# Last unit's attention values with tokens in rows, two loads cut in halves, and three PSUM banks exchanged, in a pooled-attention and cosine-gated MLP kernel

## The chip, the cores and the metric

The kernel runs on one core of a Trainium2 chip. The metric is the time of one execution on the device in microseconds; the median of several runs is taken. In the profile PE is TensorE, PEld its weight loads, DVE VectorE, ACT ScalarE, POOL GpSimd and SP the engine that issues DMAs only.

## The reference, cut to what matters

There are 8 batches, 8 heads, 576 positions of 64 dimensions. Keys and values are averaged over groups of 8 positions (72 groups), q attends to them, and the result, as 4608 tokens of 512, goes through a layer of 2048 hidden units with the activation h * cos(h).

```python
k_p = k.reshape(B, H, Sp, pool, D).mean(axis=3)
v_p = v.reshape(B, H, Sp, pool, D).mean(axis=3)
scores = scale * np.matmul(q, k_p.transpose(0, 1, 3, 2))
attn = softmax(scores)                      # max subtracted, 1e-9 in the sum
x = np.matmul(attn, v_p)                    # as [4608 tokens, 512]
h = x @ w_in                                # 512 -> 2048
out = (h * np.cos(h)) @ w_out               # 2048 -> 512
```

## The kernel before, in words

**Stages.** The tokens are cut into nine tiles of 512. A tile has an up stage (h, its cosine, the product g) and a down stage (g times w_out). The attention of batch t + 1 is computed inside the down stage of tile t; batch 0 has a prologue of its own. A batch has 576 tokens and a tile 512, so tile 1 holds the last 64 tokens of batch 0 (the unit `REST`) and the first 448 of batch 1. The order of every engine's instructions is the order in which the program writes them (`manual_schedule`); a wait stands only where data or a buffer need it.

**Units of attention.** For batches 0 and 1 a batch's first 512 tokens are four units `us[0]` to `us[3]`: two blocks of 256 tokens for heads 0 to 3, then the same for heads 4 to 7. A unit's output is two of the four 128-row chunks of `xT` (tokens along the free dimension): `us[0]` and `us[1]` fill chunks 0 and 1, `us[2]` and `us[3]` chunks 2 and 3. The up matmuls contract over these chunks (`ki`).

**Prologue (batch 0).** k, v and q are loaded in a form in which matmuls with a 0/1 matrix `groups` do the pooling: `pool_k_mm` (L178), `pool_v_mm` (L186, copied out to `vz` on DVE, L188). q is transposed on PE (L215, L216). For each unit: `scores` (PE L234, Exp on ACT L241), `sums_first` (matmuls with ones, L313, then Ln and Exp(-x) on ACT, L317 and L318, which give the inverse of the softmax's sum), `values_then` (PE L327, multiplication on DVE into `xT`, L329). `warm_up` (L527) is matmuls on constants. From batch 2 on units of 128 tokens for all heads go through `values_rows`: matmuls with the tokens in the output's rows (L296), with the sum as a 65th column, a reciprocal (L299) and a multiplication (L301) on DVE, and a transposing DMA into `xT`.

**Up stage.** `up_mm` (L354) computes pairs `fp` of 128-wide blocks of h, 8 matmuls a pair; `up_bank` gives the pair's PSUM bank; Sin on ACT (L364), product on DVE (L368). Of the first two pairs of a tile the matmuls on chunks 0 and 1 are written ahead of those on chunks 2 and 3. In tile 0 the pairs go through `banks[0]`, `banks[2]`, `banks[1]` in turn; in later tiles through `banks[0]`, `banks[2]`, `banks[1]` and the two `obanks`, in the order of pairs 0, 4, 1, 5, and so on.

**Down stage of tile 0.** 64 matmuls (L371) into four accumulators, with a list `fill` of other work and the place at which each stands: the attention of `REST` and of batch 1 (`S_` scores, `V_` values: PE L269, ACT L275 and L276, DVE L280), sums of weight blocks on DVE (`put_weights`, L387) for the later tiles' down stages, which use fewer products, and the copies of the accumulators (`down_out`, DVE L375, then stores on SP). The second accumulator pair lies in `banks[1]`; `us[3]`'s values are in `banks[0]`, and their multiplication is held back to place 57.

**Loads and pooling on POOL.** All loads of k, v, q, w_in and w_out except the first of k are issued from POOL's queue (L96, L115, L124, L130); each takes one of eight semaphores, so a load waits for the one eight before it. From batch 2 on POOL pools k and v with additions (L157, L163, L166, L169). w_in comes in four blocks of 512 columns, used by pairs 0 and 1, 2 and 3, 4 and 5, 6 and 7.

Of the kernel before, what the change touches and what calls it, by code (L numbers as in the profile page):

```python
# [10 lines left out]
BF16 = mybir.dt.bfloat16  # L11
# [9 lines left out]
def kernel(  # L21
# [9 lines left out]
    nc = tc.nc  # L31
    B, H, S, D = q.shape
# [5 lines left out]
    KCH = d_model // 128  # L38
# [10 lines left out]
    REST = (SEG[2], (0, H))  # L49
# [10 lines left out]
    msb = ctx.enter_context(tc.tile_pool(name="msb", bufs=3))  # L60
    psum = ctx.enter_context(tc.tile_pool(name="psum", bufs=1, space=bass.MemoryType.PSUM))

    w_in_sb = [wpool.tile([128, KCH, 512], BF16, name=f"w_in_sb{i}") for i in range(4)]
    w_out_sb = [wpool.tile([128, 4, d_model], BF16, name=f"w_out_sb{i}") for i in range(4)]
    xT = wpool.tile([128, KCH, n_tokens], BF16, name="xT")
    g_sb = wpool.tile([128, FFCH, TILE], BF16, name="g_sb")
# [28 lines left out]
    def load_even(dst, b, src, j0=0, j1=KCH):  # L95
        nc.gpsimd.dma_start(out=dst[:, j0:j1].rearrange("p j t d -> p j (t d)"), in_=even_view(src, b, j0, j1))  # L96
# [23 lines left out]
        q_tile(b)  # L120
        load_even(staged["q", b], b, q)

    def load_w_in(cg):
        nc.gpsimd.dma_start(  # L124
            out=w_in_sb[cg],
            in_=moe_w_in[:, cg * 512:(cg + 1) * 512].rearrange("(k p) f -> p k f", p=128))


    def load_w_out(cg):
# [88 lines left out]
    def ex_col(u, i):  # L218

        (c0, n), (h0, nh) = u  # L220
        return (i // 2 % 2 * (nh // 2) + i // 4 * 2 + i % 2) * n

    def scores(b, u, pair):
        scores_mm(b, u, pair)
        scores_exp(b, u, pair)
# [59 lines left out]
        else:  # L285
            later.append(mul)

    def values_rows(b, u, pair):

        (c0, n), (h0, nh) = u  # L290
        ex = att.pop(("ex", b, u))
        ps = pair.rearrange("p b n -> p (b n)").rearrange("p (j w) -> p j w", w=2 * 128)
        for i in range(nh):
            pj, hp = divmod(i, 2)
            v_and_sum = vz[b % 2].rearrange("p j a d -> p j (a d)")[:, pj, hp * (3 * D - 1):hp * (3 * D - 1) + D + 1]
            nc.tensor.matmul(ps[0:n, pj, hp * (D + 1):(hp + 1) * (D + 1)], lhsT=ex[:, ex_col(u, i):ex_col(u, i) + n],  # L296
                             rhs=v_and_sum)
        inv = asb.tile([128, KCH, 2], FP32, name="inv_rows", tag="inv_rows", bufs=2)
        nc.vector.reciprocal(out=inv[0:n], in_=ps[0:n, :, D:D + 2])  # L299
        x = asb.tile([128, d_model], BF16, name="x_rows", tag="x_rows", bufs=4)  # L300
        nc.vector.tensor_tensor(  # L301
            out=x[0:n].rearrange("p (j a d) -> p j a d", j=KCH, a=2),
            in0=ps[0:n, :, 0:2 * (D + 2)].rearrange("p j (a w) -> p j a w", a=2)[:, :, :, 0:D],
            in1=inv[0:n].unsqueeze(3).to_broadcast([n, KCH, 2, D]), op=mybir.AluOpType.mult)
        nc.sync.dma_start_transpose(out=xT[:, :, b * S + c0:b * S + c0 + n], in_=x[0:n])

    def sums_first(b, u, cs):

# [33 lines left out]
    def up_bank(t, fp):  # L342
        i = list(up_order(t)).index(fp)
        if t < FIRST:
            return (banks[0], banks[2], banks[1])[i % 3]
        return (banks[0], banks[2], banks[1], obanks)[i % 4 if i < 7 else 0]

    def up_mm(t, fp, k0=0, k1=KCH):

        h = up_bank(t, fp)  # L350
        for j in range(2):
            fc = 2 * fp + j
            for ki in range(k0, k1):
                nc.tensor.matmul(h[j] if h is obanks else h[:, j, :], lhsT=w_in_sb[fc // 4][:, ki, fc % 4:512:4],  # L354
                                 rhs=xT[:, ki, t * TILE:(t + 1) * TILE],
                                 start=(ki == 0), stop=(ki == KCH - 1))

# [129 lines left out]
    load_even(staged["q", 0], 0, q, 0, 2)  # L487
    load_even(staged["k", 0], 0, k, 2, 4)
    load_even(staged["q", 0], 0, q, 2, 4)
    load_even(staged["v", 0], 0, v)  # L490
    identity = consts.tile([128, 128], BF16, name="identity")
    make_identity(nc, identity)
    dist, sign = [x.rearrange("p f n -> p (f n)").bitcast(FP32)[:, 0:ROW * Sp].rearrange("p (t n) -> p t n", t=ROW)
# [13 lines left out]

    kv_even_tiles(1)
    q_tile(1)
    for cg in range(3):  # L510
        load_w_in(cg)
    load_even(staged["k", 1], 1, k)
    load_even(staged["q", 1], 1, q, 0, 2)
    load_w_in(3)
    load_even(staged["q", 1], 1, q, 2, 4)
    load_w_out(0)
    load_even(staged["v", 1], 1, v)
# [6 lines left out]
    def warm_up(n, bank):  # L524

        for i in range(n):
            nc.tensor.matmul(bank, lhsT=warm[:, 0:128], rhs=warm)  # L527
# [16 lines left out]
    for put in (q_transpose_mm(0, banks[2][:, 0, :], 9, 14), q_transpose_mm(0, obanks[0], 14, 18)):  # L544
        put(vec)
    sums_first(0, us[1], obanks[1])
    warm_up(2, banks[1][:, 0, :])
    scores(0, us[2], banks[0])
    scores(0, us[3], banks[2])
    pool_v_mm(0, banks[1], 0, 2)  # L550
    sums_first(0, us[2], banks[0][:, 0, :])
    values_then(0, us[0], obanks[1])
    pool_v_mm(0, banks[1], 2, 4)
    values_then(0, us[1], obanks[0])
    sums_first(0, us[3], banks[2][:, 0, :])
    values_then(0, us[2], obanks[1])
    values_then(0, us[3], banks[1][:, 0, :])
    up_mm(0, 0, 0, 2)
    up_mm(0, 1, 0, 2)
    sin_tables()  # L560

    for t in range(NT):
# [35 lines left out]
        def S_(n, bank):  # L598
            return lambda: scores(b, us[n], banks[bank])
# [3 lines left out]
        def V_(n, bank, wait=None):  # L603
            return lambda: values(b, us[n], banks[bank], wait)
# [5 lines left out]
        if t < FIRST:  # L610

            mms = [(ms, 4 * cg + f) for cgs, mss in (((0, 2), (0, 1)), ((0, 2), (2, 3)), ((1, 3), (2, 3, 0, 1)))
                   for cg in cgs for ms in mss for f in range(4)]
            acc = [*obanks, banks[1][:, 0, :], banks[1][:, 1, :]]
            os = [msb.tile([128, 2, d_model], FP32, name="o_two", tag="o_two", bufs=2) for _ in range(2)]
            fill = [(2, lambda: scores(t, REST, banks[1])), (2, S_(0, 0)),
                    (4, lambda: put_weights(0, nc.vector, (1,))),
                    (8, lambda: pool_v_mm(1, banks[2])), (8, lambda: values(t, REST, banks[1])),
                    (8, lambda: put_weights(0, nc.vector, (3, 2))), (8, S_(1, 0)), (9, V_(0, 2)),
                    (18, lambda: put_weights(0, nc.vector, (4,))), (20, lambda: put_weights(1, nc.vector, (1,))),  # L620
                    (20, V_(1, 0)), (28, S_(2, 2)), (35, S_(3, 0)), (36, V_(2, 2)),
                    (38, lambda: put_weights(1, nc.vector, (3, 2, 4))), (44, V_(3, 0, later)), (57, lambda: later.pop()())]
# [123 lines left out]
```

## Time and profile before

| | us |
|---|---|
| median of 3 runs | 293.5 (293.22 to 293.76) |
| profiled execution | 293.22, of which the span from first to last instruction 291.4 |
| PE busy | 275.0 (94%) |
| DVE busy | 213.0 (73%) |
| ACT busy | 168.0 (58%) |
| POOL busy | 131.6 (45%) |

An engine's busy time is the union of its instructions. The chain that ended last, followed back from the end, is 85% PE. The prologue lies from 0 to 17.3 us (the first up matmul), tile 0's up stage to 33.6, its down stage to 53.6, and tile 1's up stage begins at 59.4.

### The profile page before, as it was taken

What the parts mean: (1) busy time and instruction counts of PE and PEld (TensorE: products, weight loads), DVE (VectorE), ACT (ScalarE), POOL (GpSimd) and SP (SyncE); (2) the same over time, 40 slices, a digit from 0 to 9 for tenths busy, and PEclk for the clock granted to TensorE, in tenths of its full rate; (3) what the DMA queues carried; (4) which work ended last, traced back from release to release, by engine and by line L of the source; (5) the groups of instructions that cost most, each with busy time, mean ns of one, the idle gap of its engine ahead of it and who ended that gap; (6) DMA issues with size and microseconds to landing.
All of it is one profiled execution on the core that took longest, in us unless ns stands there. A gap on an engine that the chain in (4) does not pass through costs nothing.

```text
span 291.4 us, 5864 instructions
## 1 busy us (share of the span) xinstructions
PE 275.0 (94%) x2356; PEld 185.6 (64%) x2378; DVE 213.0 (73%) x311; ACT 168.0 (58%) x201; POOL 131.6 (45%) x146
## 2 busy tenths in 40 slices
PE   7799999389999999999999999999999999999993
PEld 2555554135786578658865886588558855885682
DVE  5358775947985897589668966896689669846972
ACT  3786797226835683569356835684567456436600
POOL 8443016992079628980898089809930000000000
PEclk9999999869999999999999999999999999999999
DMA  7999999695825989979596959794570251006014
GB/s 157 197 207 211 212 205 159 90 188 85 139 55 53 151 161 201 139 143 198 89 153 111 213 91 161 138 191 77 110 157 3 55 122 42 2 13 130 2 36 109
DMA packets 56202, 36.13 MB, mean 124 GB/s; under 512 B 35440, under 2 KB 51312, under 8 KB 56176
## 3 DMA queue, kind: packets, MB, share of 16 engines
q0 software_dynamic: 18208, 18.07, 39.1%
q1 hardware_dynamic: 37328, 17.18, 29.0%
q10 hardware_dynamic: 640, 0.52, 0.8%
q8 instruction: 18, 0.29, 0.4%
q14 instruction: 8, 0.07, 0.1%
HBM read 36.70 MB, written 9.44 MB: 158 GB/s over the span
## 4 chain that ended last, share of the span: by engine, by line
PE 85%; DVE 5%; ACT 5%; DMA 2%; issue 2%; POOL 0%; POOLq 0%
PE bank L354 38%; PE obank L431 32%; PE obank L354 5%; PE bank L234 3%; DVE w L387 2%; DMA q_b<-in_q_dram 2%; PE bank L296 2%; ACT ex L241 2%; PE bank L431 2%; DVE xT L280 2%; PE bank L269 1%; ACT v_sb L275 1%; DVE o_two L375 0%; PE obank L178 0%; DVE g_sb L368 0%
## 5 line engine op out<-in xcount | busy, mean ns | idle before, releaser
L354 PE MATMUL bank<-xT,w_in_sb 128*128 128x512 bf16 x495 | 114.6, 383 | 6.8 <-DVE xT L280 5.8
L364 ACT ACTIVATE cos<-bank,half_pi 128x1024 f32<-128x1024 f32 x64 | 70.5, 1116 | 62.7 <-PE bank L354 62.7
L354 PEld LDWEIGHTS <-w_in_sb 128*128 128x128 bf16 x576 | 65.1, 114 | 64.8 <-DVE xT L280 6.3
L368 DVE TENSOR_TENSOR g_sb<-bank,cos 128x1024 bf16<-128x1024 f32 x64 | 76.9, 1220 | 35.0 <-ACT cos L364 35.0
L157 POOL TENSOR_TENSOR half_sums<-kv_st 72x512 f32<-72x512 bf16 x48 | 53.9, 1149 | 8.2 <-DMA kv_st<-in_k_dram 7.7
L241 ACT ACTIVATE ex<-bank 72x1024 bf16<-72x1024 f32 (+1 forms) x40 | 35.0, 931 | 31.8 <-PE bank L234 31.8
L431 PEld LDWEIGHTS <-g 128*128 128x128 bf16 x512 | 47.8, 98 | 5.8
L431 PE MATMUL obank<-w,g 128*128 128x256 bf16 x368 | 42.6, 273 | 0.0
L431 PEld LDWEIGHTS <-g_sb 128*128 128x128 bf16 x384 | 36.9, 98 | 6.4
L163 POOL TENSOR_TENSOR half_sums<-half_sums 72x512 f32<-72x512 f32 x24 | 30.0, 1272 | 0.0
L431 PE MATMUL obank<-w_out_sb,g_sb 128*128 128x256 bf16 x240 | 28.9, 273 | 0.0
L397 DVE TENSOR_TENSOR g<-g_sb 128x1024 bf16<-128x1024 bf16 x32 | 21.9, 685 | 0.3
L710 POOL COPY gate<-g 1x1 bf16<-1x1 bf16 x5 | 0.9, 179 | 42.0 <-DVE inv_rows L299 42.0
L301 DVE TENSOR_TENSOR x_rows<-bank,inv_rows 128x512 bf16<-128x512 f32 x24 | 16.6, 691 | 0.8
L280 DVE TENSOR_TENSOR xT<-bank,inv 64x256 bf16<-64x256 f32 x14 | 5.9, 422 | 15.4 <-ACT inv L276 15.3
L431 PE MATMUL obank<-w_out_sb,g 128*128 128x256 bf16 x112 | 15.6, 273 | 0.0
L431 PE MATMUL obank<-w,g_sb 128*128 128x256 bf16 x128 | 15.3, 273 | 0.0
L354 PE MATMUL obank<-xT,w_in_sb 128*128 128x512 bf16 x64 | 15.1, 380 | 0.0
L234 PE MATMUL bank<-qT,kk 64*72 64x128 bf16 (+2 forms) x288 | 12.4, 222 | 0.6 <-DVE xT L280 0.5
L234 PEld LDWEIGHTS <-kk 64*72 64x72 bf16 x288 | 8.7, 111 | 5.7 <-issue 3.4
L332 ACT ACT_TABLE_LOAD x9 | 11.5, 1283 | 0.9 <-PEq L730 0.7
L335 ACT ACT_TABLE_LOAD x9 | 11.5, 1283 | 0.2
(101 smaller groups left out, 274.0 us busy)
## 6 DMA issues: line engine op xcount, KB each, us to landing
out_dram<-o_two SPq DMA_DIRECT2D x64, 128.0 KB, 2.4
kv_st<-in_v_dram POOLq DMA_DIRECT2D x8, 576.0 KB, 12.3
kv_st<-in_k_dram POOLq DMA_DIRECT2D x7, 576.0 KB, 7.7
q_b<-in_q_dram POOLq DMA_DIRECT2D x6, 576.0 KB, 7.7
w_in_sb<-in_moe_w_in_dram POOLq DMA_DIRECT2D x4, 512.0 KB, 13.9
w_out_sb<-in_moe_w_out_dram POOLq DMA_DIRECT2D x4, 512.0 KB, 18.2
q_b<-in_q_dram POOLq DMA_DIRECT2D x4, 288.0 KB, 12.6
g_sb<-in_k_dram SPq DMA_DIRECT2D x1, 576.0 KB, 3.5
```

The lines of the kernel that those rows point to most:

```text
L157: nc.gpsimd.tensor_tensor(out=s[:, h:h + 2], in0=x[:, h:h + 2, 0:4, :], in1=x[:, h:h + 2, 4:8, :], op=ADD)
L163: add(out=s[:, h:h + 4, 0:2, :], in0=s[:, h:h + 4, 0:2, :], in1=s[:, h:h + 4, 2:4, :], op=ADD)
L234: nc.tensor.matmul(pair[:Sp, bank, c:c + n].rearrange("p (g n) -> p g n", n=64), lhsT=kk[b % 2][half[r], key_slot(b, h0 + i, r), 0:Sp], rh ...
L241: nc.scalar.activation(out=ex[:, 0:nh * n].rearrange("p (a n) -> p a n", a=2), in_=pair[:Sp, :, 0:nh * n // 2], func=ACTF.Exp, scale=scale ...
L280: nc.vector.tensor_mul(out=x_out(b, u, half[hp]), in0=cols(pair[half[hp], hp, :], u), in1=cols(inv[half[1 - hp]], u))
L301: nc.vector.tensor_tensor(out=x[0:n].rearrange("p (j a d) -> p j a d", j=KCH, a=2), in0=ps[0:n, :, 0:2 * (D + 2)].rearrange("p j (a w) -> ...
L332: nc.scalar.preload_act_table_set("natural_log_exp_and_others")
L354: nc.tensor.matmul(h[j] if h is obanks else h[:, j, :], lhsT=w_in_sb[fc // 4][:, ki, fc % 4:512:4], rhs=xT[:, ki, t * TILE:(t + 1) * TILE] ...
L364: nc.scalar.activation(out=c, in_=ps, func=ACTF.Sin, bias=half_pi[:, :1])
L368: nc.vector.tensor_mul(out=o, in0=ps, in1=c)
L397: nc.vector.tensor_tensor(out=out[:, f0:f1], in0=x, in1=y, op=op)
L431: mms.append(lambda bank=bank, first=first, g=g, w=w, fc=fc, p=p: nc.tensor.matmul(bank[p], lhsT=g(fc, p), rhs=w(fc), start=(first and fc ...
```

## The change

1. **v of batch 0 in two loads**, for the first and the last four heads. The two calls of `pool_v_mm`, which already take half of the heads each, then wait for one load each. The first moves ahead of the scores of `us[2]` and `us[3]`, and the values of `us[0]` and `us[1]` ahead of the second. The two warm-up matmuls there go.
2. **`us[3]` of batch 0 with tokens in rows.** `value_rows` is the old `values_rows` without its DMA, and takes a unit of 256 tokens and four heads as two blocks of 128 tokens. `x_transpose_mm` transposes the four 128x128 blocks on PE into PSUM, and ACT copies them into `xT`. `us[3]`'s sums, its Ln and Exp, go. The first four up matmuls stand between the values and the transposes.
3. **w_in's first block in two loads** (rows of chunks 0 and 1, of chunks 2 and 3), each a tile of its own.
4. **Banks.** Tile 0's up pairs go through `banks[1]`, `banks[0]`, `banks[2]`. In its down stage `banks[0]`, `[1]`, `[2]` stand where `[2]`, `[0]`, `[1]` stood: the second accumulator pair is in `banks[2]`, `us[2]`'s values in `banks[0]`, `us[3]`'s in `banks[1]`. Later tiles keep their order of banks.

```diff
+    WIN = ((0, 0, 2), (0, 2, 4), (1, 0, 4), (2, 0, 4), (3, 0, 4))
+    w_in_sb = [wpool.tile([128, k1 - k0, 512], BF16, name=f"w_in_sb{i}") for i, (_, k0, k1) in enumerate(WIN)]
...
-    def values_rows(b, u, pair):
+    def value_rows(b, u, pair):
         (c0, n), (h0, nh) = u
+        m = min(n, 128)
...
+        for c in range(n // m):
+            for i in range(nh):
+                pj, hp = divmod(h0 + i, 2)
...
+                e0 = ex_col(u, i) + c * m
+                nc.tensor.matmul(ps[0:m, c * nh // 2 + i // 2, hp * (D + 1):(hp + 1) * (D + 1)],
+                                 lhsT=ex[:, e0:e0 + m], rhs=v_and_sum)
...
+        return x[0:m]
...
+    def x_transpose_mm(b, u, x, bank):
+
+        ps = bank.bitcast(BF16)[:, 0:512].rearrange("p (j n) -> p j n", j=2)
+        for c in range(2):
+            for j in range(2):
+                nc.tensor.matmul(ps[:, j, c * 128:(c + 1) * 128], x[:, (2 * c + j) * 128:(2 * c + j + 1) * 128],
+                                 identity, is_transpose=True)
+        return lambda copy: copy(out=x_out(b, u, slice(0, 128)), in_=ps)
...
         if t < FIRST:
-            return (banks[0], banks[2], banks[1])[i % 3]
+            return (banks[1], banks[0], banks[2])[i % 3]
...
-    load_even(staged["v", 0], 0, v)
+    load_even(staged["v", 0], 0, v, 0, 2)
+    load_even(staged["v", 0], 0, v, 2, 4)
...
-    for cg in range(3):
-        load_w_in(cg)
+    for i in range(4):
+        load_w_in(i)
     load_even(staged["k", 1], 1, k)
     load_even(staged["q", 1], 1, q, 0, 2)
-    load_w_in(3)
+    load_w_in(4)
...
     sums_first(0, us[1], obanks[1])
-    warm_up(2, banks[1][:, 0, :])
+    pool_v_mm(0, banks[1], 0, 2)
     scores(0, us[2], banks[0])
     scores(0, us[3], banks[2])
-    pool_v_mm(0, banks[1], 0, 2)
+    values_then(0, us[0], obanks[0])
+    values_then(0, us[1], obanks[1])
+    pool_v_mm(0, banks[1], 2, 4)
     sums_first(0, us[2], banks[0][:, 0, :])
-    values_then(0, us[0], obanks[1])
-    pool_v_mm(0, banks[1], 2, 4)
-    values_then(0, us[1], obanks[0])
-    sums_first(0, us[3], banks[2][:, 0, :])
-    values_then(0, us[2], obanks[1])
-    values_then(0, us[3], banks[1][:, 0, :])
+
+    x3 = value_rows(0, us[3], banks[2])
+    values_then(0, us[2], obanks[0])
     up_mm(0, 0, 0, 2)
+    x_transpose_mm(0, us[3], x3, obanks[1])(act)
     up_mm(0, 1, 0, 2)
...
-            acc = [*obanks, banks[1][:, 0, :], banks[1][:, 1, :]]
+            acc = [*obanks, banks[2][:, 0, :], banks[2][:, 1, :]]
...
-                    (20, V_(1, 0)), (28, S_(2, 2)), (35, S_(3, 0)), (36, V_(2, 2)),
-                    (38, lambda: put_weights(1, nc.vector, (3, 2, 4))), (44, V_(3, 0, later)), (57, lambda: later.pop()())]
+                    (20, V_(1, 1)), (28, S_(2, 0)), (35, S_(3, 1)), (36, V_(2, 0)),
+                    (38, lambda: put_weights(1, nc.vector, (3, 2, 4))), (44, V_(3, 1, later)), (57, lambda: later.pop()())]
```

More of the change, by code (lines that the diff above doesn't have):

```diff
@@ L61 @@
     psum = ctx.enter_context(tc.tile_pool(name="psum", bufs=1, space=bass.MemoryType.PSUM))
-    w_in_sb = [wpool.tile([128, KCH, 512], BF16, name=f"w_in_sb{i}") for i in range(4)]
+    WIN = ((0, 0, 2), (0, 2, 4), (1, 0, 4), (2, 0, 4), (3, 0, 4))
+    w_in_sb = [wpool.tile([128, k1 - k0, 512], BF16, name=f"w_in_sb{i}") for i, (_, k0, k1) in enumerate(WIN)]
     w_out_sb = [wpool.tile([128, 4, d_model], BF16, name=f"w_out_sb{i}") for i in range(4)]
@@ L121, in load_q, with load_w_in, w_in_part @@
         load_even(staged["q", b], b, q)
-    def load_w_in(cg):
+    def load_w_in(i):
+        cg, k0, k1 = WIN[i]
         nc.gpsimd.dma_start(
-            out=w_in_sb[cg],
-            in_=moe_w_in[:, cg * 512:(cg + 1) * 512].rearrange("(k p) f -> p k f", p=128))
+            out=w_in_sb[i],
+            in_=moe_w_in[k0 * 128:k1 * 128, cg * 512:(cg + 1) * 512].rearrange("(k p) f -> p k f", p=128))
+    def w_in_part(fc, ki):
+        i = fc // 4 + 1 if fc >= 4 else ki // 2
+        return w_in_sb[i][:, ki - WIN[i][1], fc % 4:512:4]
     def load_w_out(cg):
@@ L286, in values @@
             later.append(mul)
-    def values_rows(b, u, pair):
+    def value_rows(b, u, pair):
         (c0, n), (h0, nh) = u
+        m = min(n, 128)
         ex = att.pop(("ex", b, u))
         ps = pair.rearrange("p b n -> p (b n)").rearrange("p (j w) -> p j w", w=2 * 128)
[L293 to L297, printed above, removed]
+        for c in range(n // m):
+            for i in range(nh):
+                pj, hp = divmod(h0 + i, 2)
+                v_and_sum = vz[b % 2].rearrange("p j a d -> p j (a d)")[:, pj, hp * (3 * D - 1):hp * (3 * D - 1) + D + 1]
+                e0 = ex_col(u, i) + c * m
+                nc.tensor.matmul(ps[0:m, c * nh // 2 + i // 2, hp * (D + 1):(hp + 1) * (D + 1)],
+                                 lhsT=ex[:, e0:e0 + m], rhs=v_and_sum)
@@ L298, in values_rows @@
         inv = asb.tile([128, KCH, 2], FP32, name="inv_rows", tag="inv_rows", bufs=2)
-        nc.vector.reciprocal(out=inv[0:n], in_=ps[0:n, :, D:D + 2])
+        nc.vector.reciprocal(out=inv[0:m], in_=ps[0:m, :, D:D + 2])
         x = asb.tile([128, d_model], BF16, name="x_rows", tag="x_rows", bufs=4)
         nc.vector.tensor_tensor(
-            out=x[0:n].rearrange("p (j a d) -> p j a d", j=KCH, a=2),
-            in0=ps[0:n, :, 0:2 * (D + 2)].rearrange("p j (a w) -> p j a w", a=2)[:, :, :, 0:D],
-            in1=inv[0:n].unsqueeze(3).to_broadcast([n, KCH, 2, D]), op=mybir.AluOpType.mult)
@@ L305, in values_rows @@
-        nc.sync.dma_start_transpose(out=xT[:, :, b * S + c0:b * S + c0 + n], in_=x[0:n])
+            out=x[0:m].rearrange("p (j a d) -> p j a d", j=KCH, a=2),
+            in0=ps[0:m, :, 0:2 * (D + 2)].rearrange("p j (a w) -> p j a w", a=2)[:, :, :, 0:D],
+            in1=inv[0:m].unsqueeze(3).to_broadcast([m, KCH, 2, D]), op=mybir.AluOpType.mult)
+        return x[0:m]
+    def values_rows(b, u, pair):
+        (c0, n), _ = u
+        nc.sync.dma_start_transpose(out=xT[:, :, b * S + c0:b * S + c0 + n], in_=value_rows(b, u, pair))
@@ L353, in up_mm @@
             for ki in range(k0, k1):
-                nc.tensor.matmul(h[j] if h is obanks else h[:, j, :], lhsT=w_in_sb[fc // 4][:, ki, fc % 4:512:4],
+                nc.tensor.matmul(h[j] if h is obanks else h[:, j, :], lhsT=w_in_part(fc, ki),
                                  rhs=xT[:, ki, t * TILE:(t + 1) * TILE],
@@ L613 @@
                    for cg in cgs for ms in mss for f in range(4)]
-            acc = [*obanks, banks[1][:, 0, :], banks[1][:, 1, :]]
+            acc = [*obanks, banks[2][:, 0, :], banks[2][:, 1, :]]
             os = [msb.tile([128, 2, d_model], FP32, name="o_two", tag="o_two", bufs=2) for _ in range(2)]
-            fill = [(2, lambda: scores(t, REST, banks[1])), (2, S_(0, 0)),
+            fill = [(2, lambda: scores(t, REST, banks[2])), (2, S_(0, 1)),
                     (4, lambda: put_weights(0, nc.vector, (1,))),
-                    (8, lambda: pool_v_mm(1, banks[2])), (8, lambda: values(t, REST, banks[1])),
-                    (8, lambda: put_weights(0, nc.vector, (3, 2))), (8, S_(1, 0)), (9, V_(0, 2)),
+                    (8, lambda: pool_v_mm(1, banks[0])), (8, lambda: values(t, REST, banks[2])),
+                    (8, lambda: put_weights(0, nc.vector, (3, 2))), (8, S_(1, 1)), (9, V_(0, 0)),
                     (18, lambda: put_weights(0, nc.vector, (4,))), (20, lambda: put_weights(1, nc.vector, (1,))),
-                    (20, V_(1, 0)), (28, S_(2, 2)), (35, S_(3, 0)), (36, V_(2, 2)),
-                    (38, lambda: put_weights(1, nc.vector, (3, 2, 4))), (44, V_(3, 0, later)), (57, lambda: later.pop()())]
+                    (20, V_(1, 1)), (28, S_(2, 0)), (35, S_(3, 1)), (36, V_(2, 0)),
+                    (38, lambda: put_weights(1, nc.vector, (3, 2, 4))), (44, V_(3, 1, later)), (57, lambda: later.pop()())]
             for n, (ms, fc) in enumerate(mms):
```

## The prediction

> **What bounds the kernel now.** I read the page first, then PE's waits, then the place of the largest wait on DVE, POOL and PE, then the clock there, and the prologue last.
>
> ```profile
> PE 275.0 (94%) x2356; PEld 185.6 (64%) x2378; DVE 213.0 (73%) x311; ACT 168.0 (58%) x201; POOL 131.6 (45%) x146
> ...
> PE 85%; DVE 5%; ACT 5%; DMA 2%; issue 2%; POOL 0%; POOLq 0%
> ```
>
> PE sets the end: busy 275.0 of 291.4 us, 85% of the chain that ended last. A gain is a PE gap closed, PE work dropped, or PE work at a better clock. PE's waits:
>
> ```profile
> PE bank L354 <- DVE xT L280: 5.8, 1, 5.8
> PE obank L527 <- DVE g L471: 1.5, 1, 1.5
> PE bank L215 <- DMA q_b<-in_q_dram: 1.1, 1, 1.1
> ```
>
> One gap is far the longest, 5.8 us ahead of an up matmul (L354). From 70 us to the end PE's list is empty, so what is saved before tile 1's up stage arrives at the end. DVE, POOL and PE around the gap (start, duration):
>
> ```profile
> 49.37 1.39 DVE L280 TENSOR_TENSOR xT<-bank,v_sb 64x512 bf16<-64x512 f32 x2 [3.44 <-ACT v_sb L276]
> 50.79 0.69 DVE L387 TENSOR_TENSOR w<-w_out_sb,w_out_sb 128x1024 bf16<-128x1024 bf16 x1
> 51.52 3.45 DVE L387 TENSOR_TENSOR w<-w,w_out_sb 128x1024 bf16<-128x1024 bf16 x1
> 55.00 1.63 DVE L387 TENSOR_TENSOR w<-w_out_sb,w 128x1024 bf16<-128x1024 bf16 x1
> 56.67 1.29 DVE L375 COPY o_two<-bank 128x512 f32<-128x512 f32 x2
> 57.99 1.39 DVE L280 TENSOR_TENSOR xT<-bank,q_sb 64x512 bf16<-64x512 f32 x2
> ```
>
> ```profile
> 51.92 2.49 POOL L163 TENSOR_TENSOR half_sums<-half_sums 72x512 f32<-72x512 f32 x2
> 54.49 2.32 POOL L166 TENSOR_TENSOR ring<-half_sums 72x512 bf16<-72x512 f32 x2
> ```
>
> ```profile
> 51.75 1.89 PE L371 MATMUL obank<-w_out_sb,g_sb 128*128 128x512 bf16 x8
> 59.43 1.04 PE L354 MATMUL bank<-xT,w_in_sb 128*128 128x512 bf16 x2 [5.80 <-DVE xT L280]
> ```
>
> PE ends tile 0's down matmuls at 53.64 and waits for DVE's last multiplication (unit us[3], to 59.38). DVE is late because two of its last three weight sums (L387), 0.69 us elsewhere, take 3.45 and 1.63: they end at 54.97 and 56.64, each 0.55 us after a POOL addition (54.41, 56.09). DVE's tail is tied to POOL's pooling of k of batch 2, and that starts when its load lands at 46.3, whatever the engines do. The clock around the gap (stretch, its length, PE, PEld, DVE, ACT, POOL busy; PEclk; DMA):
>
> ```profile
> 49.10:52.53 3.43, 3.38 (x18) 1.61 (x17) 3.08 (x4) 3.33 (x5) 3.12 (x4) 1.00 0.46 81
> 52.53:55.94 3.41, 1.11 (x6) 0.29 (x3) 3.38 (x2) 0.00 (x0) 3.33 (x3) 1.00 0.77 108
> 55.94:59.36 3.42, 0.00 (x0) 0.00 (x0) 3.34 (x5) 0.00 (x0) 3.34 (x5) 0.50 0.61 112
> 59.36:62.77 3.41, 3.34 (x8) 1.17 (x9) 1.31 (x3) 0.00 (x0) 3.41 (x4) 0.50 0.94 201
> ```
>
> The clock halves at 55.94 and is full again at 62.77. An up matmul starts every 0.427 us at half clock, every 0.216 at full; by 62.77 only 7.8 have been started.
>
> **Part 1: banks exchanged.** The first up pair of tile 1 (fp 0) writes banks[0], the second (fp 4) banks[2]. Before, us[3] stood in banks[0], so nothing could start until 59.38. After, banks[0] held us[2], read by 50.76, and the first two k-chunks of xT come from us[0], us[1] and REST, multiplied by 45.9: four matmuls follow the down matmuls directly. banks[2] holds the accumulators copied out at 56.67 to 57.96: four more start at 58.0, ahead of us[3]'s last multiplication. Eight of 64 up matmuls go into the gap; none is added. What is late next is the same multiplication, at 59.4, for chunks 2 and 3. Their worth depends on the clock, by this trace's boundaries, 3.41 us apart:
> - Clock halves at 55.94 as before and returns at 62.77: the second four run to 59.72, then 7.2 half-clock starts by 62.77: 15.2 instead of 7.8, (15.2 - 7.8) x 0.216 = 1.6 us.
> - It halves one boundary later, at 59.36: 8 + 7.8 starts, 8 x 0.216 = 1.7.
> - It halves at 55.94 but the second four bring it back at 59.36: 8 + 14.9 starts, 15.1 x 0.216 = 3.3.
> - It never halves: 8 + 15.5, 3.4.
>
> The stretch to 55.94 was 1.11 us busy (33%) and cost the clock; with four more matmuls it is about 1.7 us (50%), and a stretch of 67% (4.74 to 8.15, 2.27 us) kept it. I cannot place 50%. Moving the boundaries through the gap, with 50% as the limit, gives 2.2 to 2.8 us; I take 2.2, nearer the low pair, because those need no luck, and keep 1.6 and 3.4 as ends. The Trainium skill ("TensorE: Matmul & The Clock Gate", section "What's actually happening") has the clock go cold after at least one idle window of about 3.4 us. The trace disagrees: it halved 2.3 us after the last matmul. By the page the remaining idle spell, 54.3 to 58.0, would mostly pass at full clock and the sum would be 3.4.
>
> **Part 2: prologue.** us[3] with tokens in rows drops four ones-matmuls (0.39), Ln and Exp on ACT (0.58, 0.63), four value matmuls (0.39) and a multiplication (0.69). It adds eight narrow matmuls (the row form: 0.41 for eight), a reciprocal (0.20), a multiplication (0.69), four transposes (0.39) and an ACT copy (0.58). Sums: PE +0.0, ACT -0.6, DVE +0.2. The order counts:
>
> ```profile
> 13.57 0.69 PE L186 MATMUL bank<-kv_st,g 64*72 64x128 bf16 x18
> ...
> 14.79 0.41 PE L313 MATMUL bank<-ex,ones 72*64 72x256 bf16 x4 [0.52 <-ACT ex L241]
> ...
> 15.34 0.69 PE L186 MATMUL bank<-kv_st,g 64*72 64x128 bf16 x18
> ...
> 17.33 1.89 PE L354 MATMUL bank<-xT,w_in_sb 128*128 128x512 bf16 x7
> ```
>
> Whole v was there at 13.57. Loads of half this size ended POOL's waits at 9.51 and 10.93, 1.4 us apart, so v's first half should be there at 12.1. Pooling it then runs 12.45 to 13.15, after the sums of us[1]. Behind it in PE's queue stand the scores of us[2]: done by 13.6, and their Exp cannot start before 13.73, when ACT is free. So this new wait is hidden while the half lands by about 12.6. DVE: copy of vz 13.2, multiplications of us[0], us[1] to 15.6, second copy to 15.98; row values of us[3] on PE 16.03 (its Exp ends 15.65); values of us[2] 16.28; first four up matmuls 16.52 to 17.4; reciprocal and multiplication on DVE to 17.47; transposes 17.53; four up matmuls to 18.65; ACT copy done 18.53. Eight up matmuls are started by 18.65 against 17.33 + 8 x 0.216 = 19.06: 0.4 us gained, of which 0.15 is lost where the fourth pair, due 16 matmuls later at 22.11, waits in the same bank for the first pair's product on DVE (done 22.25, as Sin can start only after ACT's table load, 19.85). Left: 0.25.
>
> POOL issues two loads more, 0.75 each. The identity, behind the first, moves from 4.6 to 5.4; its user starts at 7.85. Everything behind on that queue is issued later but lands by the stream, which moves the same bytes. Nearest users: tile 0's fourth w_in block (landed by 28.5, used 29.6), the second w_out block issued (at 19.20, 18.5 to land: 37.7, first used 38.1). Both cover 0.25; a gain over 0.45 would meet w_out. The first w_in block's halves land by 15.2 and 16.5, used from 16.5 and 18.65. The two warm-up matmuls leave the stretch 11.57 to 14.98, but the pooling fills it.
>
> This 0.25 is worth nothing at the end: the first late weight sum would start at 50.5, inside POOL's addition ending at 50.75, and the second still meets L163. So part 2: 0, from -0.25 to +0.25.
>
> **Sum.** The profiled execution took 293.22, its span 291.4 plus 1.8 around it; the median of the runs is 293.5. 293.5 - 2.2 = 291.3, with 290.1 to 291.9 for this case.
>
> **Rivals.**
> 1. DVE gets past POOL. If the sum now at 51.52 starts at 51.3 and goes first (0.69), only the next waits for L163, to 54.41 + 0.55 = 55.0 instead of 56.64; copies and us[3] end 1.6 earlier. 291.3 - 1.6 = 289.7 (288.5 to 290.3). Against: it lost with its 51.52 to an addition stamped 51.92, so POOL held the port before its stamp. The Trainium skill ("SBUF — State Buffer", section "Who interferes with whom") says that whoever issues first has the pair for the whole instruction; by the stamps this trace shows the opposite, and by the page this rival would be the likeliest.
> 2. Slower: the prologue loses over 0.25 us. Decides: v's first half after about 12.9, with the scores of us[2], us[3] behind it on PE. The weight sum of 50.79 then misses the opening between 50.75 and 51.05, and all three go behind POOL: 54.41, 56.09, and the third meets v's pooling (L157, 56.89 to 61.37): 61.9 instead of 56.64, 5.3 lost, 3.1 after the gain: 296.6. (Slipping in ahead of L157 it loses 0.7.) Against: 0.8 us of margin on the landing.
> 3. The exchange frees nothing: tile 1's first matmuls still wait for the last write of xT: 293.5. Against: the up matmul at 17.33 started before us[3]'s multiplication (17.97), so waits on xT go by its parts.
>
> **How the numbers follow.** Forecast 0.58, rival 1 0.20, rival 2 0.12, rival 3 and small sums near nothing 0.10. 0.2% is 0.6 us, about what a measurement of this kernel can tell from no change. Faster: 0.58 + 0.20 + 0.04 of the last = 0.82; same 0.06; slower 0.12. The range takes in the forecast, rival 1 down to 289.0 and most of rival 3: 289.0 to 293.2.
>
> **What would show it.** Right: PE's 5.8 us wait splits into about 3.7 ahead of the second pair (for L375) and under 0.7 ahead of chunk 2; eight L354 matmuls stand before DVE's last L280; the two slow weight sums still end 0.55 us after POOL's additions; the up stage starts 0.2 to 0.5 us earlier. Wrong: a first L354 of tile 1 after 57; one slow weight sum only (rival 1); three, or one beyond 57 (rival 2); a wait for the load of v or w_out on PE.

## The result, and the profile after

The changed kernel takes 291.51 us (median of 6 runs, 290.1 to 292.13) against 293.49 (293.22 to 293.79): a ratio of 0.9929, 95% interval [0.9905, 0.9953]. The forecast was 291.3. The profiled execution took 292.13, the slowest of the six. Its span from the first to the last instruction is 290.0 us; the other 2.1 us lie around it, where it was 1.8 in the kernel before (291.4 of 293.22). In kernel.py of the changed version up_mm is L378, put_weights (the sums of weight blocks) L411, the values' multiplication L288, down_out (the copies of the accumulators) L399, pool_v_mm L194, scores L242, down_mm L395, value_rows L307 to L312, the transposes of us[3] L327, and POOL's additions L165, L171 and L174.

The page's first line of engines, and its chain of the end:

```profile
PE 275.0 (95%) x2359; PEld 185.5 (64%) x2380; DVE 214.8 (74%) x312; ACT 167.5 (58%) x200; POOL 132.9 (46%) x148
...
PE 81%; DMA 10%; DVE 3%; POOL 3%; ACT 1%; issue 1%; POOLq 0%
```

PE's busy time is the same 275.0, so the gain is idle time. DMA's share of the chain rises from 2% to 10%. PE's waits, longest first (total, times, longest):

```profile
PE bank L378 <- DVE o_two L399: 4.6, 1, 4.6
PE obank L552 <- DVE g L495: 1.5, 1, 1.5
PE obank L395 <- DMA w_out_sb<-in_moe_w_out_dram: 0.8, 1, 0.8
```

The 5.8 us wait for us[3]'s multiplication has become 4.6 us for the accumulators' copies, and a wait of 0.8 for the second w_out block is new. The timelines of DVE, POOL and PE around the gap (start, duration):

```profile
50.27 1.65 DVE L411 TENSOR_TENSOR w<-w_out_sb,w_out_sb 128x1024 bf16<-128x1024 bf16 x1
51.96 3.63 DVE L411 TENSOR_TENSOR w<-w,w_out_sb 128x1024 bf16<-128x1024 bf16 x1
55.62 1.63 DVE L411 TENSOR_TENSOR w<-w_out_sb,w 128x1024 bf16<-128x1024 bf16 x1
57.29 1.29 DVE L399 COPY o_two<-bank 128x512 f32<-128x512 f32 x2
58.61 1.39 DVE L288 TENSOR_TENSOR xT<-bank,v_sb 64x512 bf16<-64x512 f32 x2
```

```profile
46.89 4.49 POOL L165 TENSOR_TENSOR half_sums<-kv_st 72x512 f32<-72x512 bf16 x4 [9.15 <-DMA kv_st<-in_k_dram]
51.68 0.85 POOL L117 DMA_DIRECT2D kv_st<-in_k_dram  x1 [0.30 <-POOL half_sums L165]
52.54 2.49 POOL L171 TENSOR_TENSOR half_sums<-half_sums 72x512 f32<-72x512 f32 x2
55.11 2.32 POOL L174 TENSOR_TENSOR ring<-half_sums 72x512 bf16<-72x512 f32 x2
```

```profile
52.96 1.03 PE L378 MATMUL bank<-xT,w_in_sb 128*128 128x512 bf16 x4
58.63 4.00 PE L378 MATMUL bank<-xT,w_in_sb 128*128 128x512 bf16 x9 [4.64 <-DVE o_two L399]
```

Four up matmuls now follow the down matmuls, four more start at the copies' end. Three sums are late instead of two. They end at 51.92, 55.59 and 57.25, each 0.54 to 0.56 behind a POOL addition (51.38, 55.03, 56.71). POOL began at 46.89 instead of 46.28, so DVE's tail is 0.6 us later than before. The clock, in stretches of 3.41 us between the points at which it changes (length; PE, PEld, DVE, ACT, POOL busy; PEclk, the granted clock; DMA share and GB/s):

```profile
52.61:56.03 3.42, 1.38 (x7) 0.58 (x6) 3.38 (x2) 0.00 (x0) 3.34 (x3) 1.00 0.63 86
56.03:59.44 3.41, 0.81 (x3) 0.27 (x3) 3.33 (x5) 0.00 (x0) 3.33 (x4) 0.50 0.61 105
59.44:62.86 3.42, 3.42 (x10) 1.21 (x9) 1.85 (x3) 0.62 (x1) 3.42 (x4) 0.50 0.93 198
```

In this execution the clock halved at 56.03, and the second four up matmuls did not bring it back: the case priced at 1.6. The prologue on PE:

```profile
11.99 0.69 PE L194 MATMUL bank<-kv_st,g 64*72 64x128 bf16 x18
12.52 0.60 PE L242 MATMUL bank<-qT,kk 64*72 64x256 bf16 x8
...
15.45 0.41 PE L307 MATMUL bank<-vz,ex 72*128 72x65 bf16 x8 [0.52 <-DVE vz L196]
...
16.36 0.81 PE L378 MATMUL bank<-xT,w_in_sb 128*128 128x512 bf16 x3 [0.18 <-issue]
17.01 0.39 PE L327 MATMUL obank<-identity,x_rows 128*128 128x128 bf16 x4
```

v's first half was there when PE was ready for it. Of the first four up matmuls one has no record (its weights were loaded at 16.12). The third up pair, the 17th matmul, starts at 19.82 instead of 20.78.

### The profile page after: what moved, and what is told of

It is laid out like the page before. It is cut to its first block, busy times and chain, and to the rows that moved or that the text cites. A ratio compares the mean times of both kernels' runs of the same rounds, so it can differ in the third digit from the quotient of the medians.

```text
span 290.0 us, 5872 instructions
## 1 busy us (share of the span) xinstructions
PE 275.0 (95%) x2359; PEld 185.5 (64%) x2380; DVE 214.8 (74%) x312; ACT 167.5 (58%) x200; POOL 132.9 (46%) x148
## 4 chain that ended last, share of the span: by engine, by line
PE 81%; DMA 10%; DVE 3%; POOL 3%; ACT 1%; issue 1%; POOLq 0%
PE bank L378 34%; PE obank L455 32%; DMA w_out_sb<-in_moe_w_out_dram 7%; PE obank L378 5%; DMA w_in_sb<-in_moe_w_in_dram 3%; PE bank L242 3%; DVE w L411 2%; PE bank L307 2%; PE bank L455 2%; PE bank L395 1%; POOL kv_st L98 1%; PE bank L277 1%; PE obank L395 1%; DVE xT L288 0%; DVE o_two L399 0%
## 5 line engine op out<-in xcount | busy, mean ns | idle before, releaser
L378 PE MATMUL bank<-xT,w_in_sb 128*128 128x512 bf16 x495 | 115.3, 384 | 5.7 <-DVE o_two L399 4.6
L378 PEld LDWEIGHTS <-w_in_sb 128*128 128x128 bf16 x576 | 65.2, 114 | 63.7 <-issue 8.2
L165 POOL TENSOR_TENSOR half_sums<-kv_st 72x512 f32<-72x512 bf16 x48 | 53.9, 1148 | 9.6 <-DMA kv_st<-in_k_dram 9.2
L171 POOL TENSOR_TENSOR half_sums<-half_sums 72x512 f32<-72x512 f32 x24 | 30.0, 1269 | 0.0
L312 DVE TENSOR_TENSOR x_rows<-bank,inv_rows 128x512 bf16<-128x512 f32 x25 | 17.3, 691 | 0.9
L288 DVE TENSOR_TENSOR xT<-bank,inv 64x256 bf16<-64x256 f32 x14 | 5.9, 422 | 15.4 <-ACT inv L284 15.4
L378 PE MATMUL obank<-xT,w_in_sb 128*128 128x512 bf16 x64 | 15.1, 379 | 0.0
L242 PE MATMUL bank<-qT,kk 64*72 64x128 bf16 (+2 forms) x288 | 12.3, 221 | 0.1
L242 PEld LDWEIGHTS <-kk 64*72 64x72 bf16 x288 | 8.7, 111 | 4.7 <-issue 3.8
(102 smaller groups left out, 275.0 us busy)
```

The costliest lines, as they stand in the source:

```text
L165: nc.gpsimd.tensor_tensor(out=s[:, h:h + 2], in0=x[:, h:h + 2, 0:4, :], in1=x[:, h:h + 2, 4:8, :], op=ADD)
L171: add(out=s[:, h:h + 4, 0:2, :], in0=s[:, h:h + 4, 0:2, :], in1=s[:, h:h + 4, 2:4, :], op=ADD)
L242: nc.tensor.matmul(pair[:Sp, bank, c:c + n].rearrange("p (g n) -> p g n", n=64), lhsT=kk[b % 2][half[r], key_slot(b, h0 + i, r), 0:Sp], rh ...
L312: nc.vector.tensor_tensor(out=x[0:m].rearrange("p (j a d) -> p j a d", j=KCH, a=2), in0=ps[0:m, :, 0:2 * (D + 2)].rearrange("p j (a w) -> ...
```

## The experiments

Theory A: the gain is the exchange of banks; the prologue's head start dies where DVE's weight sums wait for POOL. Theory B: the prologue brings the gain. Theory C: both do. "The gap" is PE's wait ahead of tile 1. The kernel before ran again beside each of three groups of experiments (medians 293.46 beside e1, e2, e3 and e5; 293.92 beside e6 to e9; 293.77 beside e4 and e10 to e12), and each ratio is to the runs beside it.

**e1, the exchange alone**, in the kernel before:

```diff
     for t in range(NT):
         b = t + 1
+        if t == 1:
+            banks[:] = [banks[2], banks[0], banks[1]]
```

> The kernel before with the exchange of banks alone: from tile 1 on the three banks are renamed, so that tile 1's first pair of up matmuls goes into the bank that held us[2] and the second into the accumulators' bank; prologue and loads as before. Theory A (the whole gain comes from eight up matmuls that move ahead of us[3]'s last multiplication; the prologue's gain dies at POOL's pooling): about 291.2 us, 290.1 to 291.9 (1.6 to 3.4 less than before, by the clock); PE's 5.8 us wait becomes about 4.3 - 0.9 = 3.4 to 3.7 ahead of the second pair; DVE's late weight sums end at 55.0 and 56.6 as before. Theory B (the gain comes from the prologue): 293.5. Theory C (both add): between, about 292.5.

Measured 290.74, ratio 0.9911 [0.9885, 0.9936]: 2.7 us less. PE's longest wait and the clock:

```profile
PE bank L354 <- DVE o_two L375: 3.5, 1, 3.5
```

```profile
54.20:57.62 3.42, 0.12 (x1) 0.00 (x0) 3.35 (x4) 0.00 (x0) 3.27 (x3) 1.00 0.80 132
57.62:61.03 3.41, 3.24 (x8) 1.17 (x8) 2.78 (x5) 0.00 (x0) 3.41 (x4) 0.50 0.72 154
```

This execution's boundaries lie 1.6 us later than those of the changed kernel's. The clock halved at 57.62, just before the second four, and one stretch brought it back. Two sums are late, as before, and end at 54.75 and 56.43. Theory B falls: the exchange alone gives all of the changed kernel's gain.

**e2, everything but the exchange**, in the changed kernel:

```diff
     for t in range(NT):
         b = t + 1
+        if t == 1:
+            banks[:] = [banks[1], banks[2], banks[0]]
```

> The changed kernel with the exchange of banks undone for tile 1: from tile 1 on the banks are renamed so that the first pair's bank is again the one that held us[3]. Prologue, halved loads and tile 0 are the changed ones. Theory A: no gain, 293.5 to 294.1, since the late weight sums are tied to POOL's pooling, which starts at 46.9 with these loads instead of 46.3; PE waits 6.1 to 6.5 us ahead of tile 1's first matmul, from about 53.1 on. Theory B: 291.5. Theory C: about 292.5.

Measured 294.23 (293.08 to 295.5), ratio 1.0026 [1.0005, 1.0046]: slower by 0.15 to 1.35 us, the median 0.1 above the range of theory A.

```profile
PE bank L378 <- DVE xT L288: 5.9, 1, 5.9
```

```profile
49.92 0.69 DVE L411 TENSOR_TENSOR w<-w_out_sb,w_out_sb 128x1024 bf16<-128x1024 bf16 x1
50.64 1.52 DVE L411 TENSOR_TENSOR w<-w,w_out_sb 128x1024 bf16<-128x1024 bf16 x1
52.20 3.62 DVE L411 TENSOR_TENSOR w<-w_out_sb,w 128x1024 bf16<-128x1024 bf16 x1
```

PE waited 5.9 us ahead of tile 1, a little less than the 6.1 to 6.5 expected, although the down matmuls were through at 52.8 instead of 53.6. Theory A holds, theory C falls. In this execution, the fastest of this kernel, the first weight sum got in between two of POOL's first additions; the next two were held.

**e3, the clock kept up in the changed kernel** and **e4, in the kernel before.** The added matmuls on constants give no part of the result.

```diff
+            if t == 1:
+                warm_up(16, banks[0][:, 0, :])      # e4: warm_up(24, banks[2][:, 0, :])
             for fp in up_order(t)[0:2]:
                 up_mm(t, fp, 0, 2)
```

> The changed kernel with 16 matmuls on constants (0.216 us each, 3.5 us in all) between tile 0's last down matmul and tile 1's first up matmul, into the bank that is free there; they add no result. The gap on PE shrinks from 4.6 to about 1.2 us. If the half clock after the gap is what holds the changed kernel's profiled execution at its 1.6 us gain: no half clock around 56 to 63, 15.5 instead of 7.2 starts behind us[3]'s multiplication, 1.5 to 1.8 us less than the changed kernel's slow executions: 290.1 to 290.6, and a narrower spread of the times. If the clock does not matter, or the extra matmuls delay something: 291.5 or more.

> The kernel before with 24 matmuls on constants (5.2 us at full clock) between tile 0's last down matmul and tile 1's first up matmul, into the bank that is free there; they add no result, and no up matmul moves. What the half clock behind the 5.8 us gap costs by itself: by 3.3 us after the restart 15.5 instead of 7.8 starts, 7.7 x 0.216 = 1.7 us, so 291.8, if the half clock stands in every execution. If the clock has nothing to do with the gain: 293.5.

e3: 290.71 (290.31 to 291.44), ratio 0.9908 [0.9881, 0.9936]. e4: 292.07, ratio 0.9940 [0.9917, 0.9963]. Neither profile shows a half clock between the prologue and the end of the kernel. e4 is 1.7 us faster than the kernel before, as expected; no up matmul moved, so this is what the half clock behind the gap costs. e3 is only 0.8 us below the changed kernel's median (the intervals overlap), just above the 290.1 to 290.6 expected; its times spread over 1.1 us where the changed kernel's spread over 2.0. The changed kernel does not pay for two stretches of half clock in every execution: its mean granted clock was 0.985 or 0.986 in three of the six, the profiled one among them, and 0.990 to 0.994 in the others. e1's profile, with one stretch, has 0.990.

**e5, the weight sums early**, in the changed kernel:

```diff
-(28, S_(2, 0)), (35, S_(3, 1)), (36, V_(2, 0)),
-                    (38, lambda: put_weights(1, nc.vector, (3, 2, 4))), (44,
+(28, S_(2, 0)), (35, S_(3, 1)),
+                    (35, lambda: put_weights(1, nc.vector, (3, 2, 4))), (36, V_(2, 0)), (44,
```

> The changed kernel with the last three weight sums (put_weights of block 1, parts 3, 2, 4) moved on DVE from behind us[2]'s multiplication to ahead of it, into a spell where DVE is idle (45.2 to 48.9) and POOL has not begun to pool (46.9). Theory A (the gap is there because these sums wait for POOL): three sums of 0.69 us each at 45.2 to 47.3, accumulators copied out by 52.7, us[3] multiplied by 54.1, no gap on PE above 0.5 us, no half clock: by 62.8 some 45 up matmuls started instead of 15, 30 x 0.216 = 6.5 us less than the profiled execution of the changed kernel: 285.5 to 286.5. If the gap has another cause (the multiplication itself, ACT, the copies): 290 to 291.5. If the third sum loses the port to POOL's first addition, it ends at 51.9 and holds up us[2]'s multiplication: about 288 to 290.

Measured 285.62 (285.26 to 285.94), ratio 0.9733 [0.971, 0.9756]. DVE and PE:

```profile
45.39 0.69 DVE L411 TENSOR_TENSOR w<-w_out_sb,w_out_sb 128x1024 bf16<-128x1024 bf16 x1
46.11 0.69 DVE L411 TENSOR_TENSOR w<-w,w_out_sb 128x1024 bf16<-128x1024 bf16 x1
46.84 0.69 DVE L411 TENSOR_TENSOR w<-w_out_sb,w 128x1024 bf16<-128x1024 bf16 x1
```

```profile
51.17 1.89 PE L395 MATMUL obank<-w_out_sb,g_sb 128*128 128x512 bf16 x8
52.90 5.34 PE L378 MATMUL bank<-xT,w_in_sb 128*128 128x512 bf16 x24
```

The three sums take 0.69 each, PE has no gap and keeps its clock. The gap left by the exchange was made by the sums that wait for POOL.

**e6, the exchange with both loads halved**, **e11, with v halved alone**, **e12, with w_in halved alone** (all in the kernel before, with its order of the prologue). They ask where the changed kernel loses 0.8 us against e1 (291.51 against 290.74).

```diff
     # e1's exchange, and
-    load_even(staged["v", 0], 0, v)
+    load_even(staged["v", 0], 0, v, 0, 2)                    # e6 and e11
+    load_even(staged["v", 0], 0, v, 2, 4)
+    WIN = ((0, 0, 2), (0, 2, 4), (1, 0, 4), (2, 0, 4), (3, 0, 4))   # e6 and e12, and what uses it
```

> The kernel before with the exchange of banks and with v of batch 0 and w_in's first block in halved loads; the prologue's order of work and us[3] as before. Question: where the changed kernel loses 0.8 us against the exchange alone. Theory A (the two further loads move the landing of k of batch 2, to which POOL's pooling and so DVE's late sums are tied): k's pooling starts at 46.5 or later instead of 46.1, time 291.2 to 291.6. Theory B (the rows form and the new order in the prologue cost it): 290.7, as with the exchange alone.

> The kernel before with the exchange of banks and v of batch 0 in two loads, w_in's first block whole. The kernels with halved loads were 0.25 to 0.3% slower than their likes with whole loads, with intervals that overlap. If the halved v is the cause: 291.5 to 292, k's pooling on POOL from 46.5 or later; if not: 290.7, pooling from 46.1.

> The kernel before with the exchange of banks and w_in's first block in two loads, v of batch 0 whole. If the halved w_in is what costs 0.25 to 0.3%: 291.5 to 292, pooling from 46.5 or later; if not: 290.7, pooling from 46.1. If both this and the kernel with v halved alone stay at 290.7, the difference seen earlier was between executions, not between kernels.

Measured: e6 292.06, 0.9940 [0.992, 0.996]; e11 291.75, 0.9928 [0.990, 0.9955]; e12 291.38, 0.9931 [0.9905, 0.9956]; e1 had 0.9911. All three lie above e1, all intervals overlap its. POOL began at 46.23, 45.83 and 46.45 in their profiles, against 46.06 in e1: these do not follow the times (e11 began 0.2 us ahead of e1 and is slower), so the later landing that theory A expected does not explain them.

The record shows where part of the 0.8 us is. Each execution's time less its span was:

| kernels | loads cut in halves | us around the span, every execution |
|---|---|---|
| e1, e7 (below) | none | 1.74 to 1.84 |
| e11, e12 | one | 1.87 to 1.94 |
| changed, e6 | both | 2.07 to 2.17 |

So each load cut in two costs 0.1 to 0.2 us outside the span, and the two of them 0.3 of the 0.8. e7 has the changed prologue without the halves, so the prologue's other edits are not the cause; why the halves cost it is not shown. In the span the medians differ by 0.45 us (289.40 against 288.95), and there the clock differs too: all six executions of e1 had a mean granted clock of 0.989 to 0.994, three of six of the changed kernel 0.985 or 0.986. The spans average 289.6 in those three, and 289.0 in the other three as in e1. Whether the halves or chance brought the lower clock is not shown.

**e7, the rows and the new order with whole loads**, in the changed kernel:

```diff
-    WIN = ((0, 0, 2), (0, 2, 4), (1, 0, 4), (2, 0, 4), (3, 0, 4))
+    WIN = ((0, 0, 4), (1, 0, 4), (2, 0, 4), (3, 0, 4))
...
-    load_even(staged["v", 0], 0, v, 0, 2)
-    load_even(staged["v", 0], 0, v, 2, 4)
+    load_even(staged["v", 0], 0, v)
```

> The changed kernel with v of batch 0 and w_in's first block in whole loads again: the new order in the prologue, us[3] in rows, the exchange of banks. The first pooling of v then waits for all of v, about 13.5, with the scores of us[2] and us[3] behind it on PE: ACT's Exp of us[2] starts at 14.6 instead of 13.5, the first up matmuls 0.7 to 1.0 us later than in the changed kernel, 16.9 to 17.4. The second rival of the prediction: DVE's weight sums then come behind POOL's additions by one place more, the third past 56.9, 3 us or more lost: 294.5 to 297. Theory A (DVE is tied to POOL, whatever comes before; the sums still end 0.55 us behind POOL's additions): 290.7 to 291.5, no later than the changed kernel.

Measured 291.2 (289.99 to 291.92), ratio 0.9904 [0.9876, 0.9932]. The prologue did get late, and by more than expected:

```profile
PE bank L194 <- DMA kv_st<-in_v_dram: 1.4, 1, 1.4
```

```profile
11.37:14.78 3.41, 1.69 (x34) 1.19 (x34) 1.48 (x4) 2.53 (x5) 0.69 (x2) 1.00 1.23 205
14.78:18.19 3.41, 3.41 (x42) 2.19 (x42) 1.84 (x4) 2.26 (x4) 1.21 (x2) 0.50 1.24 206
18.19:21.61 3.42, 3.42 (x15) 1.46 (x12) 1.36 (x3) 1.29 (x3) 2.00 (x4) 0.50 1.23 207
```

PE waited 1.4 us for v where the warm-up matmuls had stood, the clock was half from 14.78 to 21.61, and tile 1's first up matmul started at 57.32 instead of 52.96. Yet the time is about the changed kernel's. DVE:

```profile
54.63 1.18 DVE L411 TENSOR_TENSOR w<-w_out_sb,w_out_sb 128x1024 bf16<-128x1024 bf16 x1
55.85 1.64 DVE L411 TENSOR_TENSOR w<-w,w_out_sb 128x1024 bf16<-128x1024 bf16 x1
57.52 0.69 DVE L411 TENSOR_TENSOR w<-w_out_sb,w 128x1024 bf16<-128x1024 bf16 x1
```

The sums began 4.4 us later than in the changed kernel but ended only 0.96 later (58.21 against 57.25); the third went ahead of v's pooling. PE's gap was 1.2 and 0.4 us and cost no clock. A prologue 4 us late used up the idle time of the gap; the 0.96 us at its end came back through the clock: by 63 us 18 of tile 1's up matmuls had started, 15 in the changed kernel's profile.

**e8, the exchange and the sums early with the old prologue**; **e9, the changed kernel with the sums early and the exchange undone**; **e10, the kernel before with the sums early and nothing else.** The edits are those of e1, e2 and e5.

> The kernel before with the exchange of banks, and the last three weight sums ahead of us[2]'s multiplication, but without the prologue's change. Here the sums would start at 45.8 and POOL's pooling at 46.1. Theory A (the sums collide with POOL): the first goes through, the second and third wait for additions. If DVE gets in between two additions, the sums end by 49.9 and the time is 286.0 to 287.5; if it is held for all four, the second ends at 51.1, the third at 54.7, us[2]'s multiplication comes behind them, and the time is 290.5 to 293. Rival (no collision; the place of the sums alone matters): 285.6, as with the prologue's change.

> The changed kernel with the three weight sums early and the exchange of banks undone. us[3]'s multiplication ends at about 54.1, and with its bank in the way tile 1's first up matmul waits for it, 1.1 us behind the last down matmul at 53.0; no half clock. Theory A: 0.9 to 1.3 us more than with the exchange (285.6): 286.5 to 286.9, so of the exchange's gain of 2.7 us only about 1 us is left once the sums are early. Rival (the exchange is worth the same 2 to 3 us everywhere): 288 to 288.6.

> The kernel before with the last three weight sums ahead of us[2]'s multiplication and nothing else. Theory A (the gap is made by the sums that wait for POOL; the exchange and the prologue only work around it): tile 1's first up matmul starts at 54.1, behind us[3]'s multiplication, 1.1 us of gap, full clock: 286.3 to 286.9, as e9 with the changed prologue. Rival (the changed prologue is what makes room ahead of POOL): 290 or more.

| | prologue | exchange | us | ratio to before |
|---|---|---|---|---|
| e5 | changed | yes | 285.62 | 0.9733 [0.971, 0.9756] |
| e8 | old | yes | 285.38 | 0.9722 [0.9692, 0.9752] |
| e9 | changed | no | 286.67 | 0.9756 [0.9733, 0.9779] |
| e10 | old | no | 287.13 | 0.9775 [0.9748, 0.9802] |

The gap that e10 keeps:

```profile
54.90 5.37 PE L354 MATMUL bank<-xT,w_in_sb 128*128 128x512 bf16 x24 [1.08 <-DVE xT L280]
```

e10 is a little above the 286.3 to 286.9 expected, and its gap is the 1.1 us expected. With the sums early the exchange is worth 1.0 (e9 to e5) and 1.8 us (e10 to e8) by the medians, 0.7 and 1.6 by the ratios, around the 1.1 us that PE waits in e9 and e10. The changed prologue gains 0.5 (e10 to e9) or loses 0.2 (e8 to e5), and all intervals of these two pairs overlap. In e8 the sums met POOL:

```profile
45.39 0.69 DVE L387 TENSOR_TENSOR w<-w_out_sb,w_out_sb 128x1024 bf16<-128x1024 bf16 x1
46.12 1.53 DVE L387 TENSOR_TENSOR w<-w,w_out_sb 128x1024 bf16<-128x1024 bf16 x1
47.68 1.53 DVE L387 TENSOR_TENSOR w<-w_out_sb,w 128x1024 bf16<-128x1024 bf16 x1
```

They took turns with POOL's first additions and ended at 49.21. us[2]'s multiplication, whose factor ACT had ready at 48.77, started 0.4 us late for it, and PE has no gap all the same. This is the first of the two outcomes expected, and a little better than its 286.0 to 287.5. e8 and e5 are 2.7% below the kernel before and about 2% below the changed kernel's median, and e8 needs no change to the prologue.

## Why the prediction was right, and where it was not

**The bound and the place: right.** The gap of 5.8 us ahead of tile 1 was where the time could come from; e1 finds all of the gain there, and from 70 us on PE's list of waits is empty in the changed kernel as well.

**The exchange, 1.6 to 3.4, taken as 2.2: right.** e1 measures 2.7. The cases differ by the clock as the sum had it: the profiled execution of the changed kernel took the case of 1.6 (half from 56.03 to 62.86), e1's a better one. That 50% of a stretch could not be placed was fair: 40% (1.38 us) cost the clock here, 46% (1.58 us) kept it in e6:

```profile
52.66:56.07 3.41, 1.58 (x8) 0.67 (x7) 3.38 (x2) 0.00 (x0) 3.33 (x4) 1.00 0.86 117
56.07:59.49 3.42, 1.12 (x5) 0.55 (x5) 3.31 (x6) 0.00 (x0) 3.34 (x4) 1.00 0.60 113
```

It was 40% and not 50% because the down matmuls ended 0.68 us earlier than before (52.96 instead of 53.64), which took busy time out of the stretch. Which case an execution takes depends on where its boundaries fall. The boundaries were at 4.74 us in the kernel before's profile, 6.42 in e1's, 7.21 in e5's, which are different places in a grid of 3.41. The Trainium skill ("TensorE: Matmul & The Clock Gate", section "What's actually happening") calls the window free-running; these runs agree.

**The prologue's gain, 0.25 us: too small.** The third pair started 0.96 us earlier. Some 0.3 of it is that execution's: us[1]'s sums already stood at 11.65 instead of 11.92, ahead of the work that the change reorders, and between 10.99 and 12.36 over all profiles. From these sums to the third pair it is 8.17 to 8.27 us in the five profiles with the changed order and v in halves, and 8.85 to 9.02 in the eight with the old order, so the prologue gains about 0.7. It came from the row values of us[3] (15.45 instead of the 16.03 worked out) and what follows them. The step that a gain over 0.45 would meet w_out was right: PE waited 0.8 us for that block (0.3 in e1, with the old prologue).

**That it is worth nothing at the end: right in kind, mis-sized.** The first weight sum ran into POOL's addition, as written, and all three ended 0.55 us behind one. But the prologue (part 2) was given -0.25 to +0.25, and e2 measures a loss of 0.15 to 1.35. Two terms were wrong. The sum kept the 1.8 us around the span as it was, and with two loads in halves it is 2.1. And it had POOL start at 46.3 whatever the engines do, and in the profiled execution it was 46.89. That start depends on when a load lands, and over all these profiles it lies between 45.8 and 47.6. With POOL's 0.6 us, 13.9 instead of 15.2 up matmuls are started by the clock's return, and the clock case of 1.6 comes to about 1.2, an estimate. The span of the profiled execution shrank by 1.4 (291.4 to 290.0) and its time by 1.1 (293.22 to 292.13), since 0.3 went around the span. What remains of the 0.8 us between the changed kernel and e1, some 0.45 in the span, goes with the granted clock of the executions; its cause stays open. That the forecast of 291.3 came within 0.2 us of the median is in part luck: the exchange brought 0.5 more than the 2.2 taken, and the prologue lost about 0.8 where nothing was taken.

**The signs.** PE's wait was expected to split into 3.7 and under 0.7, and was 4.6 and nothing: POOL's 0.6 and the larger head start lengthened the first, and the second four at half clock covered the wait for us[3]. The up stage was to begin 0.2 to 0.5 earlier and began 0.96 earlier. Signs listed as wrong came too: three slow sums, the last ending at 57.25, and PE's wait for w_out. Three slow sums did not mean rival 2 here: the text itself has the first of them start inside an addition (part 2), and the third ended behind POOL's addition of 56.71, ahead of v's pooling.

**The rivals.** Rival 1 did not occur in the changed kernel's profile; e2's profile shows its like, one sum getting through. Rival 3 is refuted by the PE row at 52.96. Rival 2's price was wrong: e7 made the prologue late by far more than its point of decision and lost nothing against the changed kernel. The price of 5.3 us had DVE held out for all four additions of v's pooling; in e7 the third sum slipped in ahead of them, which the text has in brackets at 0.7 lost, and where a sum met such additions it went in between two of them (e8). It also left out that a late PE only uses up the gap.

## What to carry to other kernels

When an engine waits long for another, follow the other's row back until its durations are longer than elsewhere: here the bank exchange saved 2.7 us beside the gap, while moving three vector sums away from GpSimd's additions cut it from 5.8 to 1.1 us alone (6.6 us saved) and removed it together with the exchange (8.5). A head start ahead of an engine tied to a transfer was worth nothing here (e2), and a delay as long as the gap cost nothing (e7). Matmuls that are moved into a gap pay more where they also shorten the half clock (1.6 or 3.3 by the sum), and which it is depends on the execution. Compare spans as well as times: a load cut in two cost 0.1 to 0.2 us that no row of the profile shows.

## What the runs showed of the hardware that was not expected

- A POOL addition can hold off a DVE sum with two inputs in SBUF (the on-chip memory) that started before the addition's own stamp. In e2 a sum started at 52.20 and an addition was stamped 52.78; the sum ended at 55.82, 0.56 behind the second addition. In between POOL was issuing a load, which alone holds nothing off: in e12 a weight sum ran its 0.69 us inside such an issue (51.23 to 51.93), and in the kernel before a sum of products (L397) at 103.42 took 0.683. What holds the sum off so early is not shown.
- A waiting DVE sum gets in between two of the first additions (e8, e2), and between the two that write `ring` (L166; L174 in the changed kernel): in the kernel before the last sum ended at 56.64, 0.55 behind the first of these (56.09). It did not get in between the two ahead of them (L163; L171) in the profiles where it was waiting there (before, changed, e1, e2): it ended behind the second. These two and the `ring` additions all read f32, so the type read is not the difference; what is, is not shown.
- In these runs narrow matmuls (64 or 72 rows or columns) did less for the clock than full ones. In e7 a stretch with 1.69 us of them (50%) halved it, and a stretch that was busy with them throughout, 14.78 to 18.19, did not bring it back; with full matmuls 46% kept it (e6) and one busy stretch restored it (e1). The two in e7 and the one in e6 were each seen in one execution.
- The time around the span grew with each load cut in two: 1.74 to 1.84 us without, 1.87 to 1.94 with one (e11, e12), 2.07 to 2.17 with two (changed, e6).
